# Scoring head pairs two by two in two PSUM tiles, in a fused sliding-window attention and gated feed-forward kernel

## The chip, the cores and the metric

The kernel runs on one core of a Trainium2 chip. The metric is the device time of one execution in microseconds (us), as a median over runs: 331.91 us for the kernel before, over 8 runs between 331.25 and 333.65. A core has five engines that run side by side: PE (TensorE, matrix products), DVE (VectorE), ACT (ScalarE), POOL (GpSimd) and SP (here a queue that issues DMA transfers). PE writes its results into PSUM, which has eight banks of 512 fp32 columns on 128 partitions; DVE and ACT read them from there. Everything else lies in SBUF.

## The reference

Attention with 8 batches, 8 heads, 576 tokens of 64 columns, a causal window of 128 tokens and a bias that falls linearly with the distance, and then a feed-forward layer over all 4608 tokens:

```python
scores = scale * np.matmul(q, k.transpose(0, 1, 3, 2))      # 8 x 8 x 576 x 576, scale 1/8
rel = pos[:, None] - pos[None, :]
bias = slopes[:, None, None] * -np.abs(rel)                 # slopes 2**-(h+1)
mask = (rel >= 0) & (rel < 128)
attn = softmax(np.where(mask, scores + bias, -1e9))
x = np.matmul(attn, v).transpose(0, 2, 1, 3).reshape(4608, 512)
h = x @ w_in                                                # 512 -> 2048
g = h * (1.0 / (1.0 + np.exp(-beta * h)))
out = g @ w_out                                             # 2048 -> 512, fp32
```

## The kernel before

**Feed-forward.** Tokens go in nine groups of 512 (TOKG). For each group an *H item* (HS, Hm, line 475) makes 128 of the 2048 hidden columns: four matmuls of 128x512 into one PSUM bank, a tanh on ACT (sig, line 495) and a multiply on DVE (gT, line 496) that reads the same bank again, since h times the sigmoid is half of h times (1 + tanh). Sixteen H items fill gT. An *output item* (OS, line 505) is four matmuls of 128x512 that add up four of the sixteen hidden blocks for 128 tokens; four items make one output tile of 512 columns, which is halved into SBUF (osb, on DVE for groups 0 and 1, else on ACT) and stored. OG(g, i) names the four items of tile i in group g.

**Attention.** The 512 columns of x are eight heads; heads are taken in pairs p of two, one on partitions 0 to 63 and one on 64 to 127 of the transposed q and k (QK). Queries and keys go in blocks of 128, the fifth of 64 (q-block qb, key block kb). From batch 2 on, a *score visit* SC(b, m, p) (line 391) covers key blocks 0 and 1 (m = 0) or 2, 3 and 4 (m = 1) for one head pair: four or six matmuls that contract over 64 rows, both heads next to each other on the two halves of the rows, into the two-bank tile SS. ACT takes the exponential of all 1024 columns (pt, line 411), and DVE multiplies by the falling factors of the bias and the mask (factor, lines 158 and 163). PV(b, qb, g) (line 423) then makes four heads of the output of one q-block: up to eight matmuls of 65 columns (the 65th is the sum of the weights), and DVE's reciprocal and multiply (norm, line 325) give xn. X(b, qb) (line 447) transposes xn into XT, the feed-forward's input: on PE for batches up to 3, with a DVE copy, and by DMA from batch 4 (XDMA).

**The first two batches** are done in an opening (from line 599) with another layout: SP_ scores in SS and in a second two-bank tile SX, PVP outputs, XP transposes, and the last 64 tokens of a batch separately: TT, SCT (scores) and PV(b, 4, g). idle(n) issues matmuls of zeros[...]. falls_rows and falls_tail copy factor tables on DVE.

**PSUM.** SS has two banks; psum_h, two banks that rotate, holds H items (tag hps); psum_t, two, holds transposes and PV; SX two, and when the opening is over, psum_o with two rotating banks (tag ops) in their place, for output tiles and, in groups 1 and 2, for some H items (FOUR). A tile that is used again waits for the last reader of the bank it gets.

**Loads.** q, k and v come as fp32 by DMA on SP (get), POOL casts them to bf16 (cast_qk, cast_v), and SP issues a DMA transpose of q and k into QK (DT, line 378). Both queues work in order. Stores of groups 0 and 1 are issued on POOL, those of later groups on ACT, the last ones on SP (store, line 528).

**Order.** PE, SP and POOL follow the program's order; outside the opening, ACT's and DVE's is chosen by a scheduler when the program is built. From batch 2 on the attention is a list of steps with weights (att, line 570): a visit weighs 3 (5 for batch 2, m = 0), a PV 2, an X 2 or, by DMA, 0. merged mixes the visits of one half with the outputs of the half before. spread (line 715) runs a group's H and output items and, after each, as many steps as keeps the weights in proportion; need gives, for each group, the steps that the next one needs. The steps end two items ahead of the end of group 1, three in group 2, and seven from group 3 on (line 780). After each item, a finished output tile is stored.

Of the kernel before, what the change touches and what calls it, by code (L numbers as in the profile page):

```python
# [15 lines left out]
P = 128  # L16
# [3 lines left out]
def kernel(  # L20
# [65 lines left out]
    psum_t = ctx.enter_context(tc.tile_pool(name="psum_t", bufs=2, space=bass.MemoryType.PSUM))  # L86
# [5 lines left out]
    late, gates = {}, {}  # L92
# [154 lines left out]

    def TP(b, p):
        src = staged.pop((b, "p", p))
        for i in (1, 0):  # L250
            tps = psum_t.tile([P, FULL], BF16, name="tps", tag="t")
# [63 lines left out]
    def room(b, shape):  # L315

        if b == 0:
            return psum_h.tile(shape, F32, name="pvh", tag="hps")[:]
        if "o" in late:
            return late["o"].tile(shape, F32, name="pvo", tag="ops")[:]  # L320
        return psum_t.tile(shape, F32, name="pv", tag="t")[:]
# [69 lines left out]
    def SC(b, m, p):  # L391
        assert all((b, sb) in moved for sb in range((3, 5)[m]))
        qk = QK[b % 2]
        for kb in ((0, 1), (2, 4, 3))[m]:
            at, then = COLS[kb]
            nq = {3: P + 64, 4: 64}.get(kb, 2 * P)
            for e in range(2):
                o = SS[:, e, at : at + min(nq, 512 - at)]
                if kb in (0, 2):
                    o = bass.AP(  # L400
                        tensor=o.tensor, offset=o.offset,
                        ap=[list(o.ap[0]), [then - at, 2], [1, P]],
                    )
                nc.tensor.matmul(  # L404
                    o,
                    lhsT=qk[64 * e : 64 * e + 64, 1, p, P * kb : P * kb + P],
                    rhs=qk[64 * e : 64 * e + 64, 0, p, P * kb : P * kb + nq],
                    start=True, stop=True, skip_group_check=True,
                )
        pt = pt_pool.tile([P, 2, 512], BF16, name="pt", tag="pt")  # L410
        nc.scalar.activation(out=pt[:], in_=SS[:], func=ACTF.Exp, scale=qscale)  # L411
        factor(pt, m, p)
        pts[b, m, p] = pt
# [9 lines left out]
    def PV(b, qb, g):  # L423
# [6 lines left out]
        if b:  # L430
            pv = psum_t.tile([P, 4, 66], F32, name="pv", tag="t")
        else:
            pv = late["o"].tile([P, 4, 66], F32, name="pvo", tag="ops")
# [12 lines left out]

    def X(b, qb):
        nq = ROWS[qb]
        xnv = xns.pop((b, qb))[:].rearrange("p h d -> p (h d)")
        if b >= XDMA:  # L450
# [6 lines left out]
            return  # L457
        xt = psum_t.tile([P, NDM, P], BF16, name="xt", tag="t")
# [5 lines left out]
        tok0 = (b * S + P * qb) % XTR  # L464
        n1 = min(nq, XTR - tok0)
# [9 lines left out]
    def Hm(g, j, cs):  # L475
# [3 lines left out]
        if cs[0] == 0:  # L479
            if g == 0 and j in (0, 3):  # L480
                hs[g, j] = SX[:, j // 2]
            elif j % 2 and j < FOUR.get(g, 0):
                hs[g, j] = late["o"].tile([P, DM], F32, name="hpo", tag="ops")[:]
# [331 lines left out]
```

## Time and profile before

| | us |
|---|---|
| median of 8 runs | 331.91 (331.25 to 333.65) |
| the profiled execution's own time | 331.82 |
| its span, first to last instruction | 330.0 |
| PE busy in the span | 314.5 |
| DVE, ACT, POOL busy | 198.2, 186.8, 91.6 |

By stage, from the stage table of the trace (cut at the first H item of a group):

| stage | us | PE busy | DVE busy | ACT busy |
|---|---|---|---|---|
| 0 to 50, opening and group 0 | 50.0 | 43.04 | 36.53 | 36.86 |
| 50 to 96, group 1 | 46.0 | 44.58 | 28.65 | 21.20 |
| 96 to 127, group 2 | 31.0 | 30.40 | 24.03 | 18.59 |
| 127 to 161, group 3 | 34.0 | 33.60 | 20.62 | 20.73 |
| 161 to 194, group 4 | 33.0 | 32.52 | 21.10 | 20.58 |
| 194 to 227, group 5 | 33.0 | 32.25 | 18.89 | 18.43 |
| 227 to 260, group 6 | 33.0 | 32.79 | 20.78 | 20.59 |
| 260 to 291, group 7 | 31.0 | 30.79 | 16.28 | 15.38 |
| 291 to 330, group 8 and the last tiles | 39.0 | 34.51 | 11.30 | 14.49 |

In a row of the stage table, after the two times of the stretch and its length, come the busy times of PE, PEld, DVE, ACT and POOL with their counts, the granted clock of PE as a share, and the share and rate of the DMA engines. In a row of the timeline come start, time, engine, line, operation, out<-in, shape and count; neighbours of one line and tile are merged, and brackets show idle time ahead of the row and what ended it. Matmuls overlap, so the time from one row's start to the next is what a row holds PE for, not its own length; some matmul records are missing, so a count of 7 can be 8. In the list of waits come the waiting engine and line, what ended the wait, the total in us, the count and the longest.

### The profile page before, as it was taken

The numbers are of one execution on the slowest core, as the hardware profiler recorded it, in microseconds if no ns is written. First come the engines' busy times: TensorE is split into PE (matmuls) and PEld (weight loads), VectorE is DVE, ScalarE is ACT, GpSimd is POOL, SyncE is SP. The second block draws the span as 40 slices with busy tenths as digits, with TensorE's granted clock in tenths as the row PEclk, the third lists the DMA queues.
The fourth block names the chain that finished last, engine by engine and source line by source line (L and its number), as shares of the span: only waits on it lengthen the run. The fifth ranks groups of instructions, "written<-read, shape, count | busy, mean of one in ns | idle before, by whom it ended". The sixth has DMA issues, their size and how long they took to land.

```text
span 330.0 us, 6005 instructions
## 1 busy us (share of the span) xinstructions
PE 314.5 (95%) x2252; PEld 150.5 (46%) x2294; DVE 198.2 (60%) x424; ACT 186.8 (57%) x265; POOL 91.6 (28%) x150
## 2 busy tenths in 40 slices
PE   7888979999989999999999999999999999999995
PEld 3444544443544454444444444444444445444443
DVE  6686777555659874866288627662877267334500
ACT  6858868615428744676476745664676465345511
POOL 4865811334554342533313221322000000000000
PEclk9999999999999999999999999999999999999999
DMA  7999999999999999899869895997022101210021
GB/s 221 257 256 233 186 196 207 183 189 194 246 209 240 203 219 239 177 207 227 193 119 215 170 231 126 203 181 163 18 64 57 64 16 50 59 62 33 5 93 64
DMA packets 147822, 51.80 MB, mean 157 GB/s; under 512 B 135360, under 2 KB 143824, under 8 KB 147792
## 3 DMA queue, kind: packets, MB, share of 16 engines
q1 hardware_dynamic: 139152, 38.29, 62.4%
q0 software_dynamic: 4864, 6.29, 9.7%
q10 hardware_dynamic: 3776, 6.83, 5.7%
q8 instruction: 18, 0.29, 0.4%
q14 instruction: 12, 0.10, 0.1%
HBM read 36.71 MB, written 9.44 MB: 140 GB/s over the span
## 4 chain that ended last, share of the span: by engine, by line
PE 69%; DMA 13%; SPq 9%; DVE 2%; ACT 2%; issue 2%; POOL 1%; ACTq 0%; POOLq 0%; DVEq 0%
PE ops L514 30%; PE hps L488 29%; DMA fst<-in_v_dram 6%; SPq L194 5%; PE SS L404 4%; DMA fst<-in_k_dram 3%; PE pv L441 2%; SPq L382 2%; DMA fst<-in_q_dram 2%; DMA qkT<-bst 2%; SPq L205 2%; PE pv L437 2%; PE hpo L488 1%; DVE gT L496 1%; ACT pt L411 1%
## 5 line engine op out<-in xcount | busy, mean ns | idle before, releaser
L514 PE MATMUL ops<-W,gT 128*128 128x512 bf16 (+1 forms) x574 | 136.1, 373 | 1.8 <-issue 0.6
L488 PE MATMUL hps<-XT,W 128*128 128x512 bf16 x511 | 131.5, 379 | 2.0 <-DVE gT L496 0.7
L496 DVE SCALAR_TENSOR_TENSOR gT<-sig,hps 128x512 bf16<-128x512 bf16 x133 | 90.3, 683 | 68.2 <-ACT sig L495 67.2
L495 ACT ACTIVATE sig<-hps,beta_h 128x512 bf16<-128x512 f32 x133 | 91.1, 688 | 61.5 <-PE hps L488 55.0
L514 PEld LDWEIGHTS <-gT 128*128 128x128 bf16 x592 | 54.1, 98 | 58.3 <-issue 3.0
L488 PEld LDWEIGHTS <-W 128*128 128x128 bf16 x576 | 50.6, 97 | 55.7 <-issue 5.7
L411 ACT ACTIVATE pt<-SS 128x1024 bf16<-128x1024 f32 x48 | 48.9, 1019 | 20.4 <-PE SS L404 20.4
L230 POOL CAST vs<-fst 128x512 bf16<-128x512 f32 (+1 forms) x40 | 26.3, 658 | 56.4 <-DMA fst<-in_v_dram 52.6
L524 ACT ACTIVATE osb<-ops 128x512 f32<-128x512 f32 (+1 forms) x28 | 16.5, 589 | 42.9 <-PE ops L514 40.0
L215 POOL CAST bst<-fst 128x512 bf16<-128x512 f32 (+1 forms) x32 | 21.9, 685 | 57.7 <-DMA fst<-in_q_dram 47.3
L328 DVE TENSOR_TENSOR xn<-pv,zs 128x256 bf16<-128x256 f32 (+1 forms) x62 | 26.0, 420 | 1.3
L216 POOL CAST bst<-fst 128x512 bf16<-128x512 f32 (+1 forms) x32 | 20.4, 637 | 17.4 <-DMA fst<-in_k_dram 17.0
L163 DVE TENSOR_TENSOR pt<-pt,fall 128x1024 bf16<-128x1024 bf16 x24 | 18.7, 780 | 10.3 <-ACT pt L411 10.3
L158 DVE TENSOR_TENSOR pt<-pt,falls 128x1024 bf16<-128x1024 bf16 x24 | 16.9, 703 | 12.7 <-ACT pt L411 12.6
L441 PE MATMUL pv<-vs,pt 128*128 128x65 bf16 x240 | 21.6, 193 | 0.0
L441 PEld LDWEIGHTS <-pt 128*128 128x128 bf16 x240 | 16.5, 97 | 8.4
L404 PE MATMUL SS<-qkT 64*128 64x256 bf16 (+2 forms) x240 | 19.1, 252 | 0.8 <-DMA qkT<-bst 0.2
L437 PE MATMUL pv<-vs,pt 128*128 128x65 bf16 x192 | 18.1, 193 | 0.0
L437 PEld LDWEIGHTS <-pt 128*128 128x128 bf16 x192 | 15.2, 98 | 5.6
L522 DVE TENSOR_SCALAR osb<-ops 128x512 f32<-128x512 f32 (+1 forms) x9 | 5.9, 657 | 19.6 <-PE ops L514 19.6
L404 PEld LDWEIGHTS <-qkT 64*128 64x128 bf16 x240 | 8.1, 94 | 20.9 <-issue 19.0
L327 DVE RECIPROCAL zs<-pv 128x4 f32<-128x4 f32 (+1 forms) x67 | 11.1, 173 | 3.1 <-PE pv L441 2.7
(84 smaller groups left out, 181.4 us busy)
## 6 DMA issues: line engine op xcount, KB each, us to landing
fst<-in_k_dram SPq DMA_DIRECT2D x32, 256.0 KB, 5.5
fst<-in_q_dram SPq DMA_DIRECT2D x32, 256.0 KB, 5.2
fst<-in_v_dram SPq DMA_DIRECT2D x32, 256.0 KB, 4.5
out_dram<-osb ACTq DMA_DIRECT2D x26, 256.0 KB, 2.5
W<-in_moe_w_in_dram POOLq DMA_DIRECT2D x4, 512.0 KB, 8.1
W<-in_moe_w_out_dram POOLq DMA_DIRECT2D x4, 512.0 KB, 12.5
out_dram<-osb POOLq DMA_DIRECT2D x8, 256.0 KB, 3.8
fst<-in_q_dram SPq DMA_DIRECT2D x8, 128.0 KB, 3.9
```

The costliest lines, as they stand in the source:

```text
L215: nc.gpsimd.tensor_copy(out=t[0:rows, 0], in_=fs.pop(("q", b, sb))[0:rows])
L216: return nc.gpsimd.tensor_copy(out=t[0:rows, 1], in_=fs.pop(("k", b, sb))[0:rows])
L230: return nc.gpsimd.tensor_copy(out=VS[b % 2][0:rows, sb, :, 0:D], in_=fs.pop(("v", b, sb))[0:rows])
L328: nc.vector.tensor_tensor(out=xn, in0=pv[0:nq, :, 0:D], in1=zs[0:nq].broadcast_to([nq, 4, D]), op=ALU.mult)
L404: nc.tensor.matmul(o, lhsT=qk[64 * e : 64 * e + 64, 1, p, P * kb : P * kb + P], rhs=qk[64 * e : 64 * e + 64, 0, p, P * kb : P * kb + nq], ...
L411: nc.scalar.activation(out=pt[:], in_=SS[:], func=ACTF.Exp, scale=qscale)
L437: nc.tensor.matmul(pv[:, hl, 0 : D + 1], lhsT=weights(b, qb - 1, h, 1), rhs=vs[:, qb - 1, h, 0 : D + 1], start=True, stop=False,)
L441: nc.tensor.matmul(pv[:, hl, 0 : D + 1], lhsT=weights(b, qb, h, 0), rhs=vs[:, qb, h, 0 : D + 1], start=qb == 0, stop=True,)
L488: nc.tensor.matmul(hps, lhsT=W1[:, c, bass.ts(j, P)], rhs=XT[:, c, c0 : c0 + TOKG], start=(c == 0), stop=(c == NDM - 1),)
L495: gates[g, j] = nc.scalar.activation(out=sig[:], in_=hps, func=ACTF.Tanh, scale=beta_h[:, j : j + 1])
L496: gates["gT"] = nc.vector.scalar_tensor_tensor(out=gts[g][:, j, :], in0=sig[:], scalar=1.0, in1=hps, op0=ALU.add, op1=ALU.mult)
L514: nc.tensor.matmul(ops_[:, cols], lhsT=gT[:, j, i * P : i * P + P], rhs=W2[:, j, cols], start=(j == 0), stop=(j == NFF - 1),)
```

## The change

- SC takes two head pairs at a time: all matmuls of the first into one two-bank tile and of the second into another, then two exponentials and two factors. The second tile, ST, takes the banks of psum_t when the opening's last transpose is done (open_s). A pair of visits weighs twice as much.
- PV for batches from 2 on becomes PVB: eight heads of a q-block at once, in SS or ST in turn (span), with one reciprocal and one multiply over both banks. X of batches 2 and 3 also writes to SS or ST, by ordinary matmuls with the identity instead of transposes, and ACT copies it in place of DVE.
- psum_o's two banks get tags of their own, "ops" and "h3". From group 2 on, every third H item (j % 3 == 2) goes to h3. The first output tile of a group (and the third of the last group) goes to psum_h, others to "ops".
- All output tiles but the last half are halved on ACT. Stores of groups 0 and 1 are issued five items later or more.
- From group 3 on the attention's steps end eleven items ahead of the end of a group. Load jobs are no longer put directly ahead of an X by DMA.
- In the opening: calm adds three matmuls of zeros around the transposes of head pair 1; the last three falls_rows come after XP(0, 3), falls_tail after VA(0); the first half of PV(0, 4, g) takes a psum_t bank.

```diff
+    def span():
+        spans.append(spans.pop(0))
+        return spans[-1]
+
+    def obank(name, tag=None):
+        if tag is None:
+            late["n"] = late.get("n", 0) + 1
+            tag = "ops" if late["n"] % 2 else "h3"
+        return late["o"].tile([P, DM], F32, name=name, tag=tag)[:]
...
+    def calm(n):
+        z = psum_h.tile([P, 512], F32, name="z", tag="hps")
+        for _ in range(n):
+            nc.tensor.matmul(z[:], lhsT=zeros[:, 0:P], rhs=zeros[:], start=True, stop=True,
...
     def TP(b, p):
         src = staged.pop((b, "p", p))
         for i in (1, 0):
+            if (b, p) == (0, 1):
+                calm(1 + i)
...
-    def SC(b, m, p):
+    def SC(b, m, pp):
         qk = QK[b % 2]
-        for kb in ((0, 1), (2, 4, 3))[m]:
...
-        pt = pt_pool.tile([P, 2, 512], BF16, name="pt", tag="pt")
-        nc.scalar.activation(out=pt[:], in_=SS[:], func=ACTF.Exp, scale=qscale)
-        factor(pt, m, p)
-        pts[b, m, p] = pt
+        spans.sort(key=lambda t: t is not SS)
+        for p, sps in zip(pp, spans):
+            for kb in ((0, 1), (2, 4, 3))[m]:
...
+        for p, sps in zip(pp, spans):
+            pt = pt_pool.tile([P, 2, 512], BF16, name="pt", tag="pt")
+            nc.scalar.activation(out=pt[:], in_=sps[:], func=ACTF.Exp, scale=qscale)
+            factor(pt, m, p)
+            pts[b, m, p] = pt
...
-        if b:
+        if b or g == 0:
             pv = psum_t.tile([P, 4, 66], F32, name="pv", tag="t")
         else:
-            pv = late["o"].tile([P, 4, 66], F32, name="pvo", tag="ops")
+            pv = room(1, [P, 4, 66])
...
+    def PVB(b, qb):
+        pv = span()[:, :, 0 : 4 * 66].rearrange("p g (h x) -> p g h x", x=66)
+        for h in range(H):
...
+        zs = xn_pool.tile([P, 2, 4, 1], F32, name="zb", tag="zb")
+        nc.vector.reciprocal(out=zs[0:nq], in_=pv[0:nq, :, :, D : D + 1])
+        nc.vector.tensor_tensor(
+            out=xn[0:nq].rearrange("p (g h) d -> p g h d", g=2), in0=pv[0:nq, :, :, 0:D],
+            in1=zs[0:nq].broadcast_to([nq, 2, 4, D]), op=ALU.mult)
...
+        if b >= 2:
+            xt = span()[:, 0, :].rearrange("p (c q) -> p c q", c=NDM)
...
+            nc.scalar.copy(out=XT[:, :, tok0 : tok0 + n1], in_=xt[:, :, 0:n1])
...
             elif j % 2 and j < FOUR.get(g, 0):
-                hs[g, j] = late["o"].tile([P, DM], F32, name="hpo", tag="ops")[:]
+                hs[g, j] = obank("hpo", "h3" if j % 4 == 1 else "ops")
+            elif g > 1 and j % 3 == 2:
+                hs[g, j] = obank("hpo", "h3")
...
-            late[g, i] = late["o"].tile([P, DM], F32, name="ops", tag="ops")
+            if g < 2:
+                late[g, i] = obank("ops", "h3" if i % 2 and (g, i) != (1, 3) else "ops")
+            elif i == 0 or i == 2 and g == NTG - 1:
+                late[g, i] = psum_h.tile([P, DM], F32, name="oph", tag="hps")[:]
+            else:
+                late[g, i] = obank("ops", "ops")
...
-                if g < 2 or at:
+                if at:
                     nc.vector.tensor_scalar_mul(o, ops_[:, cols], 0.5)
...
-                waiting.append((row0, cols, o))
+                waiting.append((row0, cols, o, late["tick"] + (5 if g < 2 else 0)))
...
-            r += [(None, lambda g=g, qb=qb: PV(b, qb, g), 2) for g in range(2)]
+            r.append((None, lambda qb=qb: PVB(b, qb), 4))
...
-            a = [(None, lambda b=b, m=m, p=p: SC(b, m, p), w) for p in range(NP)]
+            a = [(None, lambda b=b, m=m, p=p: SC(b, m, (p, p + 1)), 2 * w) for p in (0, 2)]
...
-                while js and js[0][0] * n <= 23 * i:
+                while js and js[0][0] * n <= 23 * i and (step[0] is None or b < XDMA):
...
+            Hm(0, 0, range(3))
+            XP(0, 3)
             for h in range(5, 8):
                 falls_rows(h)
-            Hm(0, 0, range(3))
-            XP(0, 3)
-            falls_tail()
...
                 it()
-                if waiting:
+                late["tick"] += 1
+                if waiting and waiting[0][3] < late["tick"]:
                     store()
...
-                tc.tile_pool(name="psum_o", bufs=2, space=bass.MemoryType.PSUM))
+                tc.tile_pool(name="psum_o", bufs=1, space=bass.MemoryType.PSUM))
...
+        def open_s():
+            trans.close()
+            psum_s = ctx.enter_context(
+                tc.tile_pool(name="psum_s", bufs=1, space=bass.MemoryType.PSUM))
+            spans.append(psum_s.tile([P, 2, 512], F32, name="ST"))
...
-            spread(items, 0, len(items) - (7 if late_x else 3), target)
+            spread(items, 0, len(items) - (11 if late_x else 3), target)
```

## The prediction

> **What bounds the kernel now.** I read the page's busy line first, then the stage table, then who waited for whom on PE, then the timeline of one steady stretch.
>
> ```profile
> PE 314.5 (95%) x2252; PEld 150.5 (46%) x2294; DVE 198.2 (60%) x424; ACT 186.8 (57%) x265; POOL 91.6 (28%) x150
> ```
>
> ```profile
> 127.00:161.00 34.00, 33.60 (x232) 15.54 (x235) 20.62 (x42) 20.73 (x29) 12.06 (x19) 1.00 1.06 210
> 227.00:260.00 33.00, 32.79 (x236) 15.23 (x239) 20.78 (x44) 20.59 (x28) 0.61 (x1) 1.00 0.18 51
> ```
>
> In a group of 512 tokens (33 to 34 us) PE is occupied 99% of the time, DVE and ACT 60%. Nothing off PE can shorten these stages, and busy time hides bubbles, so the question is where PE's order itself loses time, and which waits a new order would add.
>
> ```profile
> PE xt L460 <- DVE xn L328: 1.4, 2, 0.8
> PE pvo L437 <- DVE xnp L328: 0.9, 1, 0.9
> PE hps L488 <- DVE gT L496: 0.7, 2, 0.4
> PE SS L404 <- DMA qkT<-bst: 0.2, 1, 0.2
> ```
>
> These are most of PE's waits after 40 us: few and short. The timeline shows what is lost without a wait:
>
> ```profile
> 204.68 1.02 PE L488 MATMUL hps<-XT,W 128*128 128x512 bf16 x4
> 205.54 1.03 PE L514 MATMUL ops<-W,gT 128*128 128x512 bf16 x4
> 206.50 0.39 PE L404 MATMUL SS<-qkT 64*128 64x256 bf16 x4
> 206.82 1.90 PE L488 MATMUL hps<-XT,W 128*128 128x512 bf16 x7
> 207.09 1.02 ACT L411 ACTIVATE pt<-SS 128x1024 bf16<-128x1024 f32 x1
> 208.00 1.45 ACT L495 ACTIVATE sig<-hps,beta_h 128x512 bf16<-128x512 f32 x2
> 209.55 1.27 DVE L496 SCALAR_TENSOR_TENSOR gT<-sig,hps 128x512 bf16<-128x512 bf16 x2
> 210.27 1.02 PE L488 MATMUL hps<-XT,W 128*128 128x512 bf16 x4 [0.45 <-DVE gT L496]
> ```
>
> From start to start, four 512-column matmuls take 0.86 us (204.68 to 205.54), but 0.96 when a score visit follows (205.54 to 206.50): entering costs 0.10. The visit holds PE for 0.32 (206.50 to 206.82), although its 4x256 columns, two halves of the rows at once (their starts lie 3 ns apart), are only two half-length steps, 0.22. So 0.10 is lost on the way in and 0.10 on the way out, 48 times. The last row is the other loss: an H bank that came free late, 0.6 us (four ops end at 208.80+0.86=209.66).
>
> **What the skill says.** The Trainium skill, "TensorEngine Tiling (Array Packing)", section Key Properties: changing the tiling mode drains TensorE, changing the tile within a mode doesn't. Scores contract over 64 rows, all else over 128, so the 0.10 at each side agrees. That a longer run in the 64-row mode pays once is shown by the tail scores:
>
> ```profile
> 41.74 0.41 PE L363 MATMUL SS<-qkT 64*128 64x64 bf16 x16
> 42.08 0.39 PE L488 MATMUL hps<-XT,W 128*128 128x512 bf16 x1
> ```
>
> Sixteen of them hold PE for 0.34: eight steps of 0.03 and one exit. The page "PSUM — Partial Sum Buffer", section on bank collisions, asks that PSUM be guarded by bank; here each tile that is reused waits for its reader (the 0.45 above), so banks decide the new waits.
>
> **The change part by part.**
>
> *Pairs of visits.* A second visit directly behind the first costs its streaming, 0.24 (starts of 0.12 per step in the trace), in place of 0.10+0.32+0.01: 0.19 saved. 24 pairs: 4.6 us. Every pair is contiguous in the built PE order.
>
> *Third H bank.* The 0.6 at 210.27 and 0.15 to 0.3 at 304.00 go: about 0.7.
>
> *Normalisation of eight heads at once, in the score tiles.* PE streams the same 65-column matmuls (0.03 each). DVE does one reciprocal (0.17) and one 512-wide multiply instead of two of 256 (0.42 each). The multiply has no row; by the 512-wide gT from PSUM I take 0.68, between 0.42 and 0.84. Hidden work either way, except when the next pair wants the tile.
>
> *Transposes of batches 2 and 3 as matmuls, copied by ACT; first-group evacuations on ACT.* Same PE columns. ACT gets 10 to 12 copies at 0.59 (the row of its XT copies) and 8 evacuations at 0.60 in place of DVE's 0.69; at 60% ACT hides them. PE's 0.79 wait for xn at 94.03 becomes one output item of 0.86 against latency 0.15, reciprocal 0.2, multiply 0.68 and release 0.05, 1.08: wait 0.2. Gain 0.5.
>
> *Two spans.* In the output stretch of group 1 the visits at 78.37 and 82.04 waited 0.2 each for the one SS (four ops took 1.18 from 77.19); 0.4 goes. The 0.3 of the split visit at 96.84/97.29, waiting for a transpose DMA, goes too, but see below.
>
> *Opening.* Three calm matmuls (0.22 each) stand ahead of transposes that wait 0.3 to 0.5 for POOL casts: 0, bounds 0 and +0.3. Three falls copies (1.5) move behind the XT copy, so the first gT and the next key copy come about 0.6 later; the PE wait of 0.63 for a POOL cast at 30.65 absorbs it. The tail output of batch 0, PV(0,4,0), takes a transpose bank and escapes the 0.9 wait at 45.6; the transpose after it stays behind DVE's chain, so I count 0.5.
>
> *Stores later on POOL.* One POOL issue (0.55) leaves the way of the casts at 80.97 to 83.7, so the loads and transposes of batch 3 on SP come up to 0.5 earlier. DMA landings of later batches lead their scores by 10 us or more (the key transposes at 136 to 144 serve scores at 161.66); the eleven items widen the lead of the XT transposes, which share SP. Stores of later groups stay on ACT. Nothing.
>
> *New waits.* In the built order, group 2 gives items 1 and 2 the same bank h3. Item 1 ends, 0.2 later its tanh (0.69), then gT (0.68), release 0.05: 1.65 against a pair of 0.67: PE waits 1.0. Queued behind it is all of PE. The pair ahead may wait for batch 3's transposes by up to 1.0; then the two waits overlap.
>
> Thirteen pairs follow another pair with an eight-head output in SS between them. The worst is in group 4. Clock from a pair's end: two H items to 1.73, output 0.48 to 2.2, output item to 3.1, H to 3.95, entry to 4.05, where the next pair wants SS. ACT: exp of the first visit starts 0.44 after the pair began (as 80.53 to 80.97), at -0.12; the second 0.90 later; it ends at 1.8. Two tanh to 3.0. DVE: two factors to 2.6, two gT to 3.7, reciprocal 3.9, multiply 4.6. PE waits 0.6. The same walk gives 0.2 in group 3, 0.1 in group 6, 0 where another item or an ST output lies between. The first X of batches 2 and 3 adds 0.3. That is 1.0+0.6+0.2+0.1+0.3=2.2; I add 0.8 for places not walked (one "ops" bank among them: its 0.60 evacuation has two H items, 1.73, as cover).
>
> Sum: 4.6+0.7+0.5+0.4+0.3+0.5-2.2-0.8=4.0 faster. The profiled execution took 331.82 (span 330.0 and 1.8 around it), 0.1 under the median of 331.91; so 327.8 and a span of 326.0.
>
> **The rivals.**
>
> *Half eaten.* Gains of 7.0 (the six terms above), but the thirteen places average 0.2 to 0.4 (2.6 to 5.2), with 1.0 for group 2 and 0.8 elsewhere as before: 329.2 to 331.8. For it: exp, exp, tanh, tanh is a burst that one SS never made. Against: ACT and DVE are 60% busy and catch up within two items.
>
> *Slower.* DVE becomes the bound where SS is used again: factors stretch to 0.9 (208.15 has 0.91, while POOL casts) and the multiply comes last in DVE's queue. With 1.8 elsewhere it decides from an average of 0.4 at the thirteen places (5.2 and 1.8 are the 7.0); at 0.6 to 0.8 they cost 7.8 to 10.4: 334 to 337. For it: one 512-wide multiply holds both banks of SS to its end. Against: the walk finds such a wait in one group of five.
>
> *The drain isn't saved*: ST is another tile and the step between visits costs as before. Gains shrink to 2.4 against 3.0: 332.4. Against: the sixteen tail matmuls.
>
> *All gain*: no wait but group 2's: 331.8-7.0+1.0=325.8.
>
> **How the numbers follow.** Forecast 0.57 (326.5 to 329.3), all gain 0.06, half eaten 0.17, drain 0.06, slower 0.14. Faster by over 0.3% (1.0 us, about what a measurement here tells from no change): 0.57+0.06+0.11=0.74; the rest of half eaten and some of the drain: same 0.11; slower 0.15. The range, 326.0 to 332.0, leaves out the slower rival and a little of the top gain.
>
> **What would show it.** Right: 24 double visits with ops or hps 0.96 in front once per pair, each pair holding PE for 0.56; no wait of PE for gT but after the first items of group 2; XT no longer copied by DVE for batches 2 and 3. Wrong: PE rows of SS or ST with idle ended by DVE xn, over 0.5 us in more than a few groups; a pair of 0.65 or more; groups 3 to 7 not shorter by 0.5 to 0.8 each.

## The result, and the profile after

The changed kernel takes 334.86 us (median of 12 runs, 333.13 to 342.81), the kernel before 331.93 (33 runs); the ratio is 1.0084, 95% interval 1.0065 to 1.0102. The longest of the 12, 342.81, ran in a slow state with a granted PE clock of 0.984, and the ratio leaves it out. The forecast was 327.8 with a range of 326.0 to 332.0. The change is slower where faster was expected, by 7.1 us against the forecast.

The page of the changed kernel, its span and its busy line:

```profile
span 333.4 us, 5966 instructions
...
PE 312.1 (94%) x2256; PEld 154.0 (46%) x2297; DVE 185.0 (55%) x346; ACT 193.8 (58%) x283; POOL 90.7 (27%) x150
```

PE's busy time fell by 2.4 us (from 314.5), yet the span grew by 3.4: idle time has come to PE. DVE became lighter and ACT heavier by what was moved, and neither is near its limit. Cut at the first H item of each group, as the two timelines show it:

| from, to | before | after | difference |
|---|---|---|---|
| start to group 2 | 95.88 | 93.32 | -2.56 |
| group 2 | 31.39 | 31.61 | +0.22 |
| group 3 | 33.43 | 37.91 | +4.48 |
| group 4 | 33.51 | 35.36 | +1.85 |
| group 5 | 32.55 | 33.59 | +1.04 |
| group 6 | 33.28 | 32.44 | -0.84 |
| group 7 | 30.44 | 30.21 | -0.23 |
| group 8 and the end | 39.52 | 38.96 | -0.56 |

The loss sits in groups 3 to 5. PE's list of waits from 60 us on (engine and line, what ended the wait, total, count, longest):

```profile
PE SS L484 <- ACT pt L438: 3.1, 1, 3.1
PE hps L549 <- DMA qkT<-bst: 2.1, 1, 2.1
PE hps L549 <- DMA XT<-xn: 2.1, 1, 2.1
PE SS L430 <- DVE xn L492: 1.1, 2, 0.6
PE hpo L549 <- DVE gT L557: 0.9, 1, 0.9
PE ST L512 <- DVE xn L492: 0.5, 2, 0.2
PE ops L580 <- ACT osb L590: 0.5, 1, 0.5
```

Rows four to six are the new waits that the prediction had walked. Rows one to three are three single waits that it did not have. They lie at three places.

**Place A, group 3.** PE's timeline:

```profile
126.75 0.39 PE L430 MATMUL SS<-qkT 64*128 64x256 bf16 x4
126.98 0.38 PE L430 MATMUL ST<-qkT 64*128 64x256 bf16 x4
127.30 1.04 PE L580 MATMUL ops<-W,gT 128*128 128x512 bf16 x4
128.17 1.03 PE L549 MATMUL hpo<-XT,W 128*128 128x512 bf16 x4
132.26 0.19 PE L484 MATMUL SS<-vs,pt 128*128 128x65 bf16 x1 [3.06 <-ACT pt L438]
...
132.97 1.90 PE L549 MATMUL hps<-XT,W 128*128 128x512 bf16 x4
134.66 1.63 PE L580 MATMUL ops<-W,gT 128*128 128x512 bf16 x4
```

The first two rows are a pair of visits: it holds PE from 126.75 to 127.30, 0.55 (0.56 was forecast). Then PE stands until 132.26 for an exponential, and afterwards four matmuls of 512 columns take 1.69 (132.97 to 134.66) where 0.86 is normal. Seven of them at some 0.42 and ten 65-column matmuls at 0.055 cost 1.7 us more: the trace's record of the clock gives PE half its rate from 132.46 to 135.87. ACT's timeline says why the exponential was late:

```profile
123.58 0.37 ACTq L598 DMA_DIRECT2D out_dram<-osb  x1
123.99 0.58 ACT L515 CAST XT<-ST 128x512 bf16<-128x512 f32 x1 [2.84 <-DMA fst<-in_v_dram]
125.13 0.60 ACT L590 ACTIVATE osb<-ops 128x512 f32<-128x512 f32 x1 [0.55 <-remote]
129.64 0.34 ACTq L598 DMA_DIRECT2D out_dram<-osb  x1
130.03 1.26 ACT L556 ACTIVATE sig<-hps,beta_h 128x512 bf16<-128x512 f32 x2 [4.30 <-DMA fst<-in_q_dram]
131.18 1.02 ACT L438 ACTIVATE pt<-SS 128x1024 bf16<-128x1024 f32 x1
```

The output tile was in SBUF at 125.73, but its store was issued at 129.64, and what ended the wait was the landing of a load of q that SP had issued at 123.25. Tanh and exponentials stood behind the store in ACT's queue for 4.3 us. A store that needs nothing from a load waited for it. The store ahead of it (123.58) had stood for a load of v, at no cost to PE.

**Places B and C, the starts of groups 5 and 6.** PE's first H item there began 2.25 and 2.29 us late (rows two and three of the waits; at group 6 the key transpose is named, but the H item reads XT, whose last transpose landed then). SP's timeline ahead of group 5:

```profile
169.30 1.21 SPq L504 DMA_TRANSPOSE XT<-xn  x1
170.56 0.58 SPq L207 DMA_DIRECT2D fst<-in_q_dram  x1
171.18 0.58 SPq L207 DMA_DIRECT2D fst<-in_k_dram  x1
171.81 0.89 SPq L207 DMA_DIRECT2D fst<-in_q_dram  x1
172.74 0.91 SPq L207 DMA_DIRECT2D fst<-in_k_dram  x1
...
190.90 1.72 SPq L504 DMA_TRANSPOSE XT<-xn  x1
192.67 1.25 SPq L207 DMA_DIRECT2D fst<-in_v_dram  x2
194.02 2.67 SPq L504 DMA_TRANSPOSE XT<-xn  x2
```

The last row is the two halves of one block of tokens: the first half is the last that group 5 reads, the second belongs to group 6. The first half landed at 194.02+4.1=198.1, and PE went on:

```profile
198.20 1.90 PE L549 MATMUL hps<-XT,W 128*128 128x512 bf16 x8 [2.09 <-DMA XT<-xn]
```

From the first XT transpose of the group to the last that it reads, SP issues 26.1 us of transfers with no pause (169.30 to 195.40). Before 169.30 it had been standing since 157.3, because that transpose waited for xn and everything behind it with it. In the kernel before, the same stretch ran from 166.80 to 191.00, 24.2 us: two more loads (0.92 and 1.14 there) stood ahead of the first transpose. And there was little to spare. SP's and PE's rows of the kernel before:

```profile
189.75 2.55 SPq L455 DMA_TRANSPOSE XT<-xn  x2
194.21 1.89 PE L488 MATMUL hps<-XT,W 128*128 128x512 bf16 x8
222.66 1.45 SPq L455 DMA_TRANSPOSE XT<-xn  x1
226.76 1.03 PE L488 MATMUL hps<-XT,W 128*128 128x512 bf16 x4
```

The last transposes that groups 5 and 6 read landed at 189.75+3.3=193.0 and 222.66+3.7=226.4, the H items began at 194.21 and 226.76: leads of 1.2 and 0.4. From that lead of 1.2 to the wait of 2.25 are 3.4 us. The longer stretch is 1.8 of them; the others are a slower landing (0.9), a first transpose that comes later in the group (0.4) and a shorter part of PE (0.4).

Places A (3.2 of gap and 1.7 of slow matmuls), B and C are 9.4 us. Without them the span is 324.0, 2.0 under the forecast of 326.0.

### The profile page after: what moved, and what is told of

Same layout as the page of the kernel before. It is cut to its first block, busy times and chain, and to the rows that moved or that the text cites. A ratio compares the mean times of both kernels' runs of the same rounds, so it can differ in the third digit from the quotient of the medians.

```text
span 333.4 us, 5966 instructions
## 1 busy us (share of the span) xinstructions
PE 312.1 (94%) x2256; PEld 154.0 (46%) x2297; DVE 185.0 (55%) x346; ACT 193.8 (58%) x283; POOL 90.7 (27%) x150
## 2 busy tenths in 40 slices
DMA packets 147821, 51.79 MB, mean 155 GB/s; under 512 B 135360, under 2 KB 143824, under 8 KB 147792
## 3 DMA queue, kind: packets, MB, share of 16 engines
q10 hardware_dynamic: 3776, 6.83, 6.3%
## 4 chain that ended last, share of the span: by engine, by line
PE 46%; DMA 29%; SPq 11%; POOL 5%; issue 3%; ACT 3%; DVE 2%; ACTq 0%; POOLq 0%; DVEq 0%
PE ops L580 15%; DMA fst<-in_k_dram 15%; PE hps L549 14%; DMA fst<-in_v_dram 9%; PE hpo L549 6%; SPq L207 6%; PE oph L580 5%; SPq L405 3%; DMA fst<-in_q_dram 3%; DMA qkT<-bst 2%; ACT pt L438 1%; PE SS L430 1%; POOL vs L243 1%; DMA XT<-xn 1%; POOL bst L229 1%
## 5 line engine op out<-in xcount | busy, mean ns | idle before, releaser
L557 DVE SCALAR_TENSOR_TENSOR gT<-sig,hps 128x512 bf16<-128x512 bf16 x99 | 66.8, 682 | 80.2 <-ACT sig L556 79.8
L580 PE MATMUL ops<-W,gT 128*128 128x512 bf16 (+1 forms) x448 | 108.2, 373 | 1.1 <-ACT osb L590 0.5
L549 PE MATMUL hps<-XT,W 128*128 128x512 bf16 x379 | 97.8, 382 | 5.4 <-DMA qkT<-bst 2.1
L556 ACT ACTIVATE sig<-hps,beta_h 128x512 bf16<-128x512 f32 x99 | 67.2, 690 | 44.1 <-PE hps L549 38.8
L549 PE MATMUL hpo<-XT,W 128*128 128x512 bf16 x168 | 43.5, 379 | 1.0 <-DVE gT L557 0.9
L556 ACT ACTIVATE sig<-hpo,beta_h 128x512 bf16<-128x512 f32 x43 | 29.7, 690 | 17.3 <-PE hpo L549 15.5
L557 DVE SCALAR_TENSOR_TENSOR gT<-sig,hpo 128x512 bf16<-128x512 bf16 x43 | 29.3, 682 | 11.6 <-ACT sig L556 11.2
L438 ACT ACTIVATE pt<-SS 128x1024 bf16<-128x1024 f32 x24 | 24.5, 1019 | 11.5 <-PE SS L430 11.3
L580 PE MATMUL oph<-W,gT 128*128 128x512 bf16 x126 | 29.2, 379 | 0.1
L438 ACT ACTIVATE pt<-ST 128x1024 bf16<-128x1024 f32 x24 | 24.5, 1022 | 0.0
```

Of the source, the lines that this page charges most:

```text
L438: nc.scalar.activation(out=pt[:], in_=sps[:], func=ACTF.Exp, scale=qscale)
L549: nc.tensor.matmul(hps, lhsT=W1[:, c, bass.ts(j, P)], rhs=XT[:, c, c0 : c0 + TOKG], start=(c == 0), stop=(c == NDM - 1),)
L556: gates[g, j] = nc.scalar.activation(out=sig[:], in_=hps, func=ACTF.Tanh, scale=beta_h[:, j : j + 1])
L557: gates["gT"] = nc.vector.scalar_tensor_tensor(out=gts[g][:, j, :], in0=sig[:], scalar=1.0, in1=hps, op0=ALU.add, op1=ALU.mult)
L580: nc.tensor.matmul(ops_[:, cols], lhsT=gT[:, j, i * P : i * P + P], rhs=W2[:, j, cols], start=(j == 0), stop=(j == NFF - 1),)
```

## Experiments

The theory after this reading: what was forecast on PE, ACT and DVE came true, and two in-order queues took it back, ACT at a store and SP with its transposes. The main rival: the reuse of the two score tiles, or DVE, holds PE there anyway. Ratios are to the kernel before, measured at the same sitting, with 95% intervals. Its median was 331.3 to 331.7 at the sittings of the experiments and 331.93 beside the changed kernel, so up to 0.6 us of a difference between medians below can come from the sitting.

**Seven items in place of eleven.**

```diff
-            spread(items, 0, len(items) - (11 if late_x else 3), target)
+            spread(items, 0, len(items) - (7 if late_x else 3), target)
```

> The changed kernel with the attention steps of the late groups ending seven items ahead of a group's end, as before, and all else changed. Theory (SP's queue): the transposes of XT are late at the start of groups 5 and 6 (PE waits of 2.25 and 2.29 us for a DMA) because SP issues some 25 us of transfers back to back behind the first transpose of a group; stretched steps bring that first transpose later by about 1 us, so both waits grow to about 3 and a third one may appear: 335.5 to 338. Rival (the eleven crowd ACT, DVE and the reuse of the score tiles): the waits of PE for DVE and the two DMA waits shrink, 331 to 333.

333.92 us, 1.0097 (1.0059 to 1.0135). That is less than the 335.5 to 338 expected. At the group starts PE waits 2.9 and 2.4: B grew, C did not, no third wait came. ACT still stands 3.2 at the store, but with another order of steps PE loses 1.4 there, with no slow matmuls behind it; instead PE has half its rate for 3.4 us behind B. So eleven is not what made B and C; it shortened B by 0.6.

**Loads allowed ahead of an XT transpose again.**

```diff
-                while js and js[0][0] * n <= 23 * i and (step[0] is None or b < XDMA):
+                while js and js[0][0] * n <= 23 * i:
```

> The changed kernel with loads allowed directly ahead of a transpose of XT again, as before the change; all else changed. Theory (SP's queue): two loads, 1.8 us of SP's issue, stand behind the first transpose of groups 4 and 5 in place of ahead of it; put ahead, the last transpose comes 1.8 us earlier and the two DMA waits fall from 2.25 and 2.29 to about 0.5 each: 331 to 332. Rival (DMA engines or the data are late, not the order of the queue): waits stay at 2 or more, 334 to 335.5.

332.11 us, 1.0001 (0.9981 to 1.0022), 2.75 less than the changed kernel. B is gone, C is 1.8, A is still there (3.7 of idle PE). The profiled execution, 334.25, is the slowest of the 20, with half rate for 6.8 us around A, so A weighs more in it than in the median. The order of SP's queue is the cause of B. C stays, and the trace says why: that last transpose was issued at 225.84 and took 4.7 to land.

**Stores of group 2 on POOL.**

```diff
-        eng = nc.gpsimd if g < 2 else nc.sync if row0 >= B * S - 2 * P else nc.scalar
+        eng = nc.gpsimd if g < 3 else nc.sync if row0 >= B * S - 2 * P else nc.scalar
```

> The changed kernel with the four stores of group 2 issued on POOL in place of ACT. Theory (ACT stands at a store): the store's issue on ACT waits for an earlier load of batch 4; without it the idle PE time of 3.1 us in front of the eight-head output in group 3 goes, and with it the 1.7 to 2 us of half-rate matmuls behind it: 329.5 to 331. Rival (DVE or the reuse of SS would hold PE there anyway): PE waits 1 to 3 us at the same place for DVE xn: 333 to 335.

330.86 us, 1.0001 (0.9983 to 1.0019), 4.0 less than the changed kernel. The 3.1 us and the slow matmuls are gone, and B and C are 1.3 and 1.9. A new wait of 1.7 came, for DVE xn, ending at 146.07. Its cause is seen in this kernel's timelines of POOL and of DVE:

```profile
139.51 0.54 POOL L598 DMA_DIRECT2D out_dram<-osb  x1 [8.80 <-ACT osb L590]
140.05 0.62 POOL L228 CAST bst<-fst 128x512 bf16<-128x512 f32 x1
140.60 0.62 POOL L229 CAST bst<-fst 128x512 bf16<-128x512 f32 x1
141.16 0.61 POOL L228 CAST bst<-fst 128x512 bf16<-128x512 f32 x1
```

```profile
140.83 3.75 DVE L171 TENSOR_TENSOR pt<-pt,falls 128x1024 bf16<-128x1024 bf16 x2 [0.22 <-ACT pt L438]
```

POOL stood 8.8 us at a store whose tile was not ready; the casts behind it then ran without a gap, and two factors of DVE took 3.75 us beside them, where two take 1.6 (0.69 each, 0.92 apart) in the changed kernel at the same place. The Trainium skill, "SBUF — State Buffer", section "SBUF: two separate sides", says that DVE and GpSimd share one pair of ports, held for a whole instruction; the numbers agree, though no run here sets this cause apart.

**All XT transposes on PE.**

```diff
-    XDMA = 4
+    XDMA = 8
...
-            late_x = TOKG * (g + 2) > XDMA * S
+            late_x = TOKG * (g + 2) > 4 * S
```

> The changed kernel with every transpose of XT made by matmuls on PE and copied by ACT, none by a DMA from SP. 13 such transposes more on PE at 0.22 us each, 2.9 us. Theory (SP's queue is late because of the XT transposes in it): both DMA waits, 2.25 and 2.29, go, and the group starts are as PE's own work has them: 334.9-4.5+2.9 = 333.3, between 332 and 334.5. Rival (spans are the bound): the transposes take a score tile each and PE waits for it, 336 to 340.

336.07 us, 1.0145 (1.0119 to 1.0171): 2.8 more than expected, and in the rival's range. The group starts have no wait any more, as the theory said, and PE's waits at the transposes, which the rival expected, are 1.0 us in all, half of them in the changed kernel too. The edit also lets loads stand ahead of a transpose of XT again, since the condition b < XDMA now always holds. One term was miscounted: the trace has 20 such transposes more (80 matmuls), not 13, which is 4.4 us at 0.22. In the profiled execution, 335.22, group 2 begins 2.5 us later than in the changed kernel, although the edit has no transposes before it: PE waited 1.3 in the opening and then had half its rate from 11.63 to 15.05. Coming later, and with the load landed by 128.55, the store that held ACT for 4.3 at place A holds it for 0.8 here, and PE has no wait there. A wait of 1.3 at an exponential in group 4 is new. The cause of the rest stays open, so this run speaks for the group starts and not for the price of the transposes.

**Both queues mended**: the loads' order as in the second run, and two stores of group 2 on POOL.

```diff
-        eng = nc.gpsimd if g < 2 else nc.sync if row0 >= B * S - 2 * P else nc.scalar
+        eng = nc.gpsimd if row0 < 2 * TOKG + 2 * P else nc.sync if row0 >= B * S - 2 * P else nc.scalar
```

> The changed kernel with two things at once: loads allowed ahead of the transposes of XT as before, and the two stores of group 2 that ACT issues at the start of group 3 issued on POOL (the other two of the group stay on ACT, since POOL stood 8.8 us at one of them and DVE's two factors behind it took 3.75 us). Theory (two queues, SP and ACT, ate the gain): no idle PE before the output of eight heads in group 3, no wait at the start of group 5, 1.3 to 1.9 at the start of group 6: 327 to 328.5. Rival (something else ate it and will show once these are gone, such as DVE at the reuse of SS): 330 to 332.

327.54 us (326.08 to 330.1), 0.9894 (0.9845 to 0.9942): about the forecast. In the profiled execution (span 324.3, the fastest of the four) A, B and C are all gone, C by luck: its last transpose landed 3.5 us after issue, 0.2 before PE's first H item.

**Single visits on top of that.**

```diff
-        spans.sort(key=lambda t: t is not SS)
-        for p, sps in zip(pp, spans):
+        use = [span() for _ in pp]
+        for p, sps in zip(pp, use):
...
-            a = [(None, lambda b=b, m=m, p=p: SC(b, m, (p, p + 1)), 2 * w) for p in (0, 2)]
+            a = [(None, lambda b=b, m=m, p=p: SC(b, m, (p,)), w) for p in range(NP)]
```

> The kernel with both queues mended, but score visits one by one again, turning through the two score tiles. Theory (a visit's two drains cost 0.19 and pairs save one of them 24 times): the switch losses of PE return, 4.6 us; 331.5 to 333. Rival (drains are not what pairs save; a change of tile costs the same): same as the paired kernel within 1 us.

330.78 us, 0.9974 (0.9959 to 0.9989), a little under the 331.5 to 333 expected. That is 3.2 more than with pairs by the medians and 4.9 by the spans of the profiled executions (329.2 and 324.3), where the rival had at most 1. Its PE timeline, below, shows the drains back in full: four matmuls ahead of a visit hold PE for 0.96 (200.17 to 201.13) and the visit for 0.32, as in the kernel before, so 24 times 0.19 are the 4.6. Two reuses of SS (0.7 each), which only pairs have, take 1.4 off; 1.0 more at group 2's item 2 and 0.8 at a key transpose come on top: 5.0.

```profile
200.17 1.03 PE L580 MATMUL ops<-W,gT 128*128 128x512 bf16 x4
201.13 0.39 PE L430 MATMUL ST<-qkT 64*128 64x256 bf16 x4
201.45 1.04 PE L549 MATMUL hps<-XT,W 128*128 128x512 bf16 x4
```

**Eleven alone, in the kernel before.**

```diff
-            spread(items, 0, len(items) - (7 if late_x else 3), target)
+            spread(items, 0, len(items) - (11 if late_x else 3), target)
```

> The kernel before with one edit: attention steps of the late groups end eleven items ahead of a group's end. Theory (SP's queue is near its limit before the change too, 0.4 us to spare at group 5, and eleven brings the first XT transpose some 0.5 to 1 us earlier): 331 to 332, with lane waits on ACT as the only harm. Rival (eleven itself is what makes the DMA waits): PE waits of 2 us or more for XT at the starts of groups 5 and 6, 335 to 337.

332.12 us, 1.0022 (1.0007 to 1.0038): no wait for a DMA at any group start, no stall at a store for a load. Eleven is nearly neutral, and by itself it widens the leads of the last XT transposes at groups 5 and 6 from 1.2 and 0.4 to 2.7 and 1.7.

**The planner as before, all else changed**: the edits of the first two runs together.

```diff
-                while js and js[0][0] * n <= 23 * i and (step[0] is None or b < XDMA):
+                while js and js[0][0] * n <= 23 * i:
...
-            spread(items, 0, len(items) - (11 if late_x else 3), target)
+            spread(items, 0, len(items) - (7 if late_x else 3), target)
```

> The changed kernel with both edits of the planner undone: attention steps end seven items ahead, and loads may stand directly ahead of a transpose of XT. Stores as changed. Theory (the order of SP's queue made the DMA waits, the eleven items with the new order made ACT's store meet a lane of loads that are under way): no wait at a store, as with seven alone; the DMA waits at groups 5 and 6 are between those of seven alone (2.9 and 2.4) and those of the order restored at eleven (0 and 1.8), so about 1 and 1.5: 329.5 to 331.5. Rival (the stall at the store comes with any order of the loads but that of seven alone): a wait of 3 us in group 3, 333 to 335.

332.47 us (328.65 to 333.74), 0.9996 (0.9968 to 1.0024). That is over the 329.5 to 331.5 expected. ACT stands 2.9 at the store after all and PE loses 1.1 to it; the waits at the group starts are 2.5 and 2.0, and PE has half its rate for 3.4 us behind the first. My account of A by the eleven items fell with this run and the first: ACT's stall is there with seven as well.

**The early stores at once.**

```diff
-                waiting.append((row0, cols, o, late["tick"] + (5 if g < 2 else 0)))
+                waiting.append((row0, cols, o, late["tick"] + 0))
```

> The changed kernel with the stores of groups 0 and 1 issued on POOL at once, not five items later; all else changed. Theory (the later stores on POOL play no part in the loss): the same three waits and 333.5 to 335.5. Rival (they move the casts on POOL and with them the loads that ACT's store waits for): the wait of 3.1 us in group 3 changes by over 1 us, 331 to 333.5 or above 336.

331.04 us, 0.9991 (0.9973 to 1.0008), 3.8 less than the changed kernel. This is the rival's outcome: the later stores on POOL, which the theory held to be innocent, bring the stall. Without them ACT's second store of group 2 goes out at once (osb at 126.56, store at 127.19). In the built program every DMA of SP and ACT takes the next of eight semaphores in turn, and waits until the transfer that had it before has landed. Stores leave one list, oldest first, so late stores of groups 0 and 1 also put those of group 2 later in the program, behind more loads. In the changed kernel the store got the semaphore of batch 4's first load of q (number 106 for both in the trace; the load landed at 129.56, the store was issued at 129.64), in this run that of a load of v issued much earlier (landed at 121.11). B and C are 1.8 and 1.6 here.

**One store moved, to shift that turn by one.**

```diff
-        eng = nc.gpsimd if g < 2 else nc.sync if row0 >= B * S - 2 * P else nc.scalar
+        eng = nc.gpsimd if row0 < 2 * TOKG + P else nc.sync if row0 >= B * S - 2 * P else nc.scalar
```

> The changed kernel with one store, the first of group 2, issued on POOL in place of ACT; the stores of groups 0 and 1 stay late. In the built program each DMA from SP or ACT takes the next of eight lanes in turn and waits until the transfer that had the lane before has landed; with one store fewer the second store of group 2 comes to stand on the lane of a 64-row load of v (issued at 122.6 in the changed kernel, waited for by nobody after 126.9) in place of that of the first load of q of batch 4 (landed at 129.56). Theory (the lane is what holds ACT): ACT waits for 0 to 1.5 us there, PE's 3.1 us in group 3 falls to under 0.5: 330.5 to 331.8. Rival (the late stores on POOL hold ACT or the casts in another way): the 3 us stay, 334 to 335.5.

331.07 us, 0.998 (0.9962 to 0.9999). ACT's timeline of this kernel:

```profile
125.06 0.60 ACT L590 ACTIVATE osb<-ops 128x512 f32<-128x512 f32 x1 [2.00 <-remote]
127.78 0.37 ACTq L598 DMA_DIRECT2D out_dram<-osb  x1
128.20 1.27 ACT L556 ACTIVATE sig<-hps,beta_h 128x512 bf16<-128x512 f32 x2 [2.54 <-DMA fst<-in_v_dram]
```

The same store now waits for the load that has the neighbouring turn, of v and not of q, and for 2.5 us in place of 4.3; that load landed at 127.70, 0.8 later than I had set. PE loses 1.5 (1.3 by the list of waits), and no slow matmuls follow. The stores of groups 0 and 1 are as late as in the changed kernel, so it is the shared turn that holds ACT.

**The two edits undone, nothing else.**

```diff
-                while js and js[0][0] * n <= 23 * i and (step[0] is None or b < XDMA):
+                while js and js[0][0] * n <= 23 * i:
...
-                waiting.append((row0, cols, o, late["tick"] + (5 if g < 2 else 0)))
+                waiting.append((row0, cols, o, late["tick"] + 0))
```

> The changed kernel with two edits undone: stores of groups 0 and 1 at once, and loads allowed directly ahead of a transpose of XT. Everything that the prediction counted as gain or new wait on PE, ACT and DVE is kept. Theory (these two edits hold the whole difference between forecast and result; 3.8 for the first alone, 2.75 for the second alone): 327.3 to 328.8, about the 327.8 forecast. Rival (they don't add, since one stall hides the other's): 329 to 331.

329.29 us, 0.9939 (0.9916 to 0.9962): by the medians 5.6 of the 7.1 us, and 4.9 when each kernel is set against the kernel before of its own sitting. That is over the 327.3 to 328.8 expected and in the rival's range: apart the two edits gave 2.75 and 3.8, together less than their sum. A and B are gone; C is 2.1 in the profiled execution, whose last transpose was issued 0.4 later in the group than in the run with both queues mended and landed after 5.1 us and not 3.5. Half rate for 3.4 us behind C costs 1.6 more there. What is left is C: the change shortens PE's part of group 5 (32.55 before, 31.28 where nothing waits), and SP's part had 0.4 to spare. So the two edits hold most of the difference, not all.

**Loads drawn forward, so that SP works while it stood.** The run with both queues mended, and:

```diff
-                while js and js[0][0] * n <= 23 * i:
+                while js and js[0][0] * n <= 23 * i + (6 * n if b >= XDMA - 1 else 0):
...
-            elif g > 1 and j % 3 == 2:
+            elif g > 1 and j % 3 == 2 and (g, j) != (2, 2):
```

> The kernel of the run before this one, with the loads and key transposes of the next batch drawn six ticks forward from batch 3 on, so that SP issues eight loads and two transposes ahead of a group's first XT transpose, where it stood idle for some 7 us; and item 2 of group 2 in another bank than item 1. Theory (SP's back-to-back chain behind the first XT transpose is what binds the group starts): the wait at group 6 goes (-1.3 to -1.9) and the 1.0 at group 2's item 2 goes: 324.5 to 326. Rival (casts on POOL bunch up at the group starts and stretch DVE's factors): PE waits for DVE xn of 1 us or more in several groups, 327 to 331.

326.27 us (326.0 to 326.48), 0.9847 (0.9831 to 0.9863). No wait at the start of groups 3 to 8, and none at group 2's item 2. A wait of 1.5 for DVE xn came in group 3, so the gain was smaller than expected; the ratio's interval overlaps that of the run with both queues mended, and what is clear is that the waits are gone.

**The same from batch 4 on.**

```diff
-                while js and js[0][0] * n <= 23 * i + (6 * n if b >= XDMA - 1 else 0):
+                while js and js[0][0] * n <= 23 * i + (6 * n if b >= XDMA else 0):
```

> The kernel with loads drawn six ticks forward, but from batch 4 on in place of batch 3, so that the casts on POOL don't bunch up beside DVE's factors in group 3 (PE waited 1.5 us there for DVE xn, 0.7 without the drawing forward). Theory (bunched casts slow DVE): the wait in group 3 falls to 0.7, 325.0 to 326.2. Rival (no connection): 1.5 stays, 326.0 to 326.6.

325.85 us, 0.9823 (0.9793 to 0.9853). The wait fell to 0.7 as expected, but not for the reason given. ACT's timeline of the run before it, the one with the wait:

```profile
139.55 0.37 ACTq L598 DMA_DIRECT2D out_dram<-osb  x1
140.02 0.69 ACT L556 ACTIVATE sig<-hpo,beta_h 128x512 bf16<-128x512 f32 x1 [1.17 <-DMA fst<-in_k_dram]
```

ACT had again stood 1.2 us at a store, for a load of k. In the later run the store went out without such a wait. Casts stretched one factor to 0.98 and account for 0.3 at most.

**The tile used longest ago first.**

```diff
-        spans.sort(key=lambda t: t is not SS)
```

> As the run before it, and a pair of visits takes the score tile that was used longest ago first, where the changed kernel always takes SS first. Theory (PE's waits for DVE xn at SS are of the tile that was just written by an output of eight heads): the two waits of 0.7 to 1.1 fall to 0.2 or less each; 324.0 to 325.5. Rival (they only move to the second visit of the pair, 0.24 us later): 0.2 to 0.5 less than the run before it.

325.16 us (324.93 to 326.94), 0.9807 (0.9776 to 0.9837). The waits did not go: one row of its PE timeline shows that they moved to the second visit of the pair, as the rival had it,

```profile
144.91 0.40 PE L429 MATMUL SS<-qkT 64*128 64x256 bf16 x6 [0.68 <-DVE xn L491]
```

and the 0.7 us to the run before lie within the intervals. By its median it is the fastest of all, 6 us under the kernel before and 10 under the changed one. Its page:

```profile
span 323.5 us, 6008 instructions
...
PE 312.6 (97%) x2297; PEld 152.8 (47%) x2297; DVE 185.1 (57%) x346; ACT 194.0 (60%) x283; POOL 94.1 (29%) x152
```

PE is as busy as in the changed kernel (312.1) in 9.9 us less. The last transposes that groups 5 and 6 read landed at 185.3 and 217.9, 5.6 and 4.3 before the H items at 190.91 and 222.19. The traffic is the same in both kernels, 51.79 MB, so the amount to be moved does not by itself make the waits.

## Why the prediction was wrong

The signs on PE, ACT and DVE were right; the queues of DMAs were not walked.

- *Pairs of visits*, 4.6: right. A pair holds PE for 0.55 (0.56), and single visits bring back 0.96 and 0.32; the run with single visits lost 3.2 by the medians and 4.9 by the profiled spans, so the total is less sure than the price of one pair.
- *X wait*, *two spans*, *opening*: with the four pairs of group 1 (0.8) the terms forecast some 2.2 up to group 2, and the profiled execution gained 2.56. The size is uncertain: other profiled kernels with the changed opening begin group 2 at 93.1 to 94.8, one at 95.8, against 93.32 here. X waits 0.2 twice, as walked. One of the two 0.2 of *two spans* stayed.
- *Third H bank*: the 0.6 before an H item in group 5 is gone.
- *New waits*: 0.9 to 1.0 at group 2's item 2 (1.0 forecast), 0.5 in group 3 (0.2), 0.7 in group 4 (0.6), nothing to see in group 6 (0.1). The 0.8 for places not walked was not needed. The multiply over eight heads took 0.686 (0.68) and the reciprocal 0.20.
- **The step that failed is the paragraph on the later stores on POOL, which ends "Nothing."** It says that landings "lead their scores by 10 us or more", that "the eleven items widen the lead of the XT transposes, which share SP", and that "Stores of later groups stay on ACT". Each holds as far as it goes, and none of them carries "Nothing":
  - The lead of 10 us is that of the key transposes. That of the XT transposes was never read, and was 1.2 and 0.4 us at groups 5 and 6 in the kernel before. Eleven items alone do widen it, by 1.5 and 1.3, but the order of the load jobs, an edit listed with the change, got no price at all. It put two loads, 1.8 us, behind the first transpose; slower landings and, at group 6 above all, PE's shorter group (by 1.3) did the rest. The runs show B gone when the order is restored, and B and C both gone when SP is given more to do ahead of the first transpose.
  - The stores stayed on ACT, but took other turns at the shared semaphores. 4.3 us of ACT, 3.2 of PE and 1.7 of slow matmuls came from one store. Undoing the later stores takes 3.8 us off by the medians (3.1 by the ratios), though the prediction priced only the 0.55 us of POOL that they free.
  - Both edits undone give back 4.9 to 5.6 of the 7.1 us. The rest goes with place C, where PE's own gain met a lead of 0.4.
- The time fell into the rival *Slower* (334 to 337), but not by its mechanism: PE waits for DVE xn are 1.6 us in all in the changed kernel, and its two places of SS were never over 0.7. They reach 1.5 and 1.7 only where ACT or POOL had first stood at a store. It was the right time for a wrong reason. Its chance, 0.14, was too low mainly because no case had a queue of transfers as the bound.
- "Groups 3 to 7 not shorter by 0.5 to 0.8 each" was named as a sign of a wrong forecast, and it came: groups 3, 4 and 5 grew and group 7 gained 0.2. The signs of a right one came as well (a pair holds PE for 0.55, 0.96 in front once, XT copied by ACT), since they looked at PE and DVE alone.

Each queue that a moved transfer passes counts. The same views of the kernel before would have shown it: SP's timeline between the first and last XT transpose of a group, without a pause, and the last landing beside PE's next H item.

## What to carry to other kernels

When PE's work between two meetings with a queue gets shorter, look up how early the last transfer of that queue lands; its lead, not the queue's share of busy time, says how much can be gained. Look for the first instruction at which the queue stands still and what is parked behind it: work that needs nothing can go ahead of it. Here that took the last wait at a group start away; the medians fell by 1.3 to 1.7 us with it and one changed bank, which is not clear of noise. A store issued from a computing engine's queue can hold that engine for a load issued elsewhere, if both take turns at the same semaphores, so after any move of a DMA read what ends that engine's waits.

## What the runs showed of the hardware

- The same DMA transpose of XT, issued within 0.5 us of the same point of a group, landed after 3.5, 4.7 and 5.1 us in three kernels. At a lead of under 1 us such a spread decides alone whether PE waits.
- PE's rate can fall to half behind a wait: at place A 65-column matmuls went from 0.029 to 0.055 at 132.47, and the wait of 3.2 us cost 4.9. The length of the wait alone does not decide it. The traces' record of the clock shows half rate for 3.41 us behind waits of 1.98 (the two edits undone), 2.36 (the planner as before), 2.69 (seven items) and 3.06 us (place A), for 6.83 us around one of 3.52 (loads allowed ahead), and full rate behind 2.09 and 2.13 us (places B and C) and 2.19 us (seven items, group 6). Within a trace the drops lie whole multiples of 3.41 us after the record's first change; at 1.98 PE had stood for 2.1 of the 3.41 us that end with the drop, while the 2.13 lay across two such stretches, at most 2.0 in one. That fits these traces and was not tested by a run of its own. The Trainium skill, "TensorE: Matmul & The Clock Gate", part on the HAM clock gate, gives half the clock after an idle window of about 3.4 us. The length of 3.4 agrees; that PE must stand for all of it does not, since 1.98 was enough, and the measurement decides.
- Casts on POOL without a gap stretched two factors on DVE from 1.6 to 3.75 us.
